# Attention with a memory state, then 128 chosen rows through two layers: full-array reads, a row of scores by way of DRAM, and two batches turned by VectorE

## The chip, the cores and the metric

The kernel runs on one core of a Trainium2 chip. A core has TensorE (matrix products, called PE in the profile), VectorE (DVE), ScalarE (ACT), GpSimd (POOL) and SyncE (SP), each with its own queue of instructions that it takes in order, and 16 DMA engines that they share. The metric is the device time of one execution in microseconds; the median of the runs counts.

## The reference

```
B, H, S, Ns, D = 8, 8, 512, 32, 64                  # all float32
scores = x @ state^T / 8                            # (B,H,512,32)
a  = softmax(scores) over the 32;   xread = a  @ state      # (B,H,512,64)
scores2 = state @ x^T / 8                           # (B,H,32,512)
a2 = softmax(scores2) over the 512; sread = a2 @ x          # (B,H,32,64)
X = concat(xread, sread) over rows, heads side by side      # (B,544,512)

s = X @ w_gate                                      # (B,544)
for each batch: take the 128 rows of largest s
    y = relu(rows @ w1) @ w2                        # 512 -> 1024 -> 512
    out[rows] = rows + sigmoid(s[rows]) * y
out elsewhere = X
```

Every batch goes through a small attention in both directions (each position reads the 32 states of its head, each state reads the 512 positions), and then 128 of its 544 rows go through two layers and are written back over themselves.

## The kernel before

A batch of x is loaded into one tile `xf` (partition p holds positions 4p to 4p+3 of every head). TensorE turns it, four transposes for each pair of heads (`turn`, L340), and ScalarE copies the turned blocks out of PSUM into `xT` (`turned`, L349). With the turned states as weights, 16 small matmuls give the scores of all heads in one PSUM tile `ps_s` (L369). VectorE turns the scores in 32 by 32 blocks, takes maximum, difference, sum and product over the 32 states and turns the result back (`in`, `max`, `sub`, `sum`, `mult`, `out`, L383 to L405; ScalarE does the exponential, L393). The other direction takes its exponential straight from PSUM (L415), is turned by TensorE (L469, kept by ScalarE at L472) and is multiplied with `xf` (`sread`, L485).

The read of a position (`read`, L447) is done in four chunks c of 128 positions. A chunk is four matmuls, for two groups g of four heads and two halves i of the array: 64 rows of weights (`eT`, half i) and 129 columns of `st_v`, in which two heads stand side by side and a last column holds the state's own gate score. They fill `ps_o`, two banks, of which there is one buffer. ScalarE copies the 512 columns to the tile `xs` (`rows`, L451), and VectorE adds the four gate columns to the scores `sc` of the chunk (`gate`, L455). `xs` is stored by SP (L512), and four small stores take the state rows (L517).

The choice of a batch needs its 544 scores as a row on every partition. TensorE transposes each column of `sc` spread over 128 columns (`row`, L558, and `row_s`, L561, for the last 32), and ScalarE copies the row to `srow` (L564, L567). VectorE counts for each row how many others beat it (`win`, L577, five operations), TensorE adds what is missing (`over`, L604), VectorE turns the rank into a one-hot matrix (`oh`, L617, five operations) and TensorE picks row numbers and scores with it (`pick`, L632). GpSimd fetches the chosen rows from `out` in DRAM (`fetch`, L524), which waits for that batch's stores. The layers run for batches [0], [1, 2], [3, 4], [5, 6] and [7]: transposes (L690, kept by ScalarE at L693), first layer (L707), second layer (L724), the sum on VectorE (L727) and the put into `out` by GpSimd (L524 again).

What runs when is a fixed order, written by a planner in `carry_out` (L112). Each piece of work is given its engine, a length, the pieces it comes after, the buffers it takes or uses, and a key: the batch number plus a number of its kind from the table `LATER`. The layers have 100 added there, so that TensorE takes them only where no attention piece is ready. The planner steps through time, and on the engine that is free first it takes, of the pieces that could start within `SOON` of the first, the one with the smallest key. A transfer has a time to landing (`lands`) that those after it wait for in the plan. On the chip each engine takes its own pieces in the planned order and waits for semaphores where a real duration differs from the planned one. SP's queue holds the loads, the stores and their waits in one order.

Of the kernel before, what the change touches and what calls it, by code (L numbers as in the profile page):

```python
# [18 lines left out]
def kernel(  # L19
# [35 lines left out]
    def pool(name, bufs, **kw):  # L55
        return ctx.enter_context(tc.tile_pool(name=name, bufs=bufs, **kw))

    N_X, N_XR = 5, 8
# [4 lines left out]
    psum = pool("psum", 1, space=bass.MemoryType.PSUM)  # L63

# [5 lines left out]
    SOON = {"PE": 0.0000, "DVE": 0.4931, "ACT": 0.0000, "POOL": 1.8045, "SP": 0.3000}  # L70

    LATER = {
        "add": -100.0000, "below": 1.9500, "exp": -0.0600, "exps": -0.7084, "fetch": 0.2600, "first": 100.0000,
        "gate": -0.5600, "gate_s": 4.8280, "heads": 0.4872, "in": -1.0433, "index": -2.8646, "load": -50.0000,
        "load_x": -2.0000, "max": 4.0896, "mult": 4.3959, "numbers": 0.2545, "off": -1.9260, "oh": -2.4538,
        "out": 3.4200, "over": -2.2366, "parts": -2.6851, "pick": 0.3200, "put": -100.0000, "read": 4.9387,
        "relu": -100.0000, "row": -4.7962, "row_kept": 4.8694, "row_s": -3.1695, "row_s_kept": -0.1742,
        "rows": 5.0000, "score_s": -3.7680, "scores": -1.0816, "second": 100.0000, "sexp": -0.1370,
        "sigmoid": 0.2238, "smax": 1.1888, "sread": 1.2957, "srows": -2.7199, "ssum": 1.4281, "state_T": 0.3300,
        "state_gates": 2.6509, "states": -1.3434, "store": 4.7700, "sub": -1.8119, "sum": -4.7918,  # L80
        "tables": -4.6345, "turn": -0.1899, "turn_a": 4.0218, "turned": 4.7352, "turned_a": -5.0000,
        "twice": -2.9080, "win": 4.2491, "xg": 90.0000, "xg_kept": -100.0000,
# [15 lines left out]
    class Piece:  # L98
        def __init__(self, engine, length, fn, after, takes, uses, key, lands):
            self.engine, self.length, self.fn, self.lands = engine, length, fn, lands  # L100
            self.name, self.key = key[1], key[0] + LATER.get(key[1], 0.0)
# [10 lines left out]
    def carry_out():  # L112
# [7 lines left out]
        while left:  # L120
# [15 lines left out]
            assert ready, "the plan cannot go on"  # L136
# [19 lines left out]
    P_O = Ring("ps_o", [128, 1024], F32, 1, psum)  # L156
    P_H = Ring("ps_h", [128, 512], F32, 2, psum)
    R_X = Ring("xf", [128, H, NC, D], F32, N_X, xin)
    R_XT = sbuf("xT", [128, 2, 2, 128], 12)
# [4 lines left out]
    R_XS = sbuf("xs", [128, NC, Dm], 2)  # L164
# [32 lines left out]
    st_v = const.tile([128, B, 2, 2 * D + 1], F32, name="st_v")  # L197
# [8 lines left out]
    st_T = const.tile([128, B, 2, 128], F32, name="st_T")  # L206
# [6 lines left out]
    def state_V(lo, hi):  # L213

        for q in range(4):
            k = q % 2
            r = slice(Ns * q, Ns * (q + 1))
            nc.gpsimd.tensor_copy(out=st_v[r, lo:hi, :, D * k:D * (k + 1)], in_=st_c[r, lo:hi, :, 0])
# [572 lines left out]
```

## Time and profile before

| what | value |
|---|---|
| median of three runs | 221.9 us (221.47 to 222.27) |
| the profiled execution, its own time | 222.47 us |
| its span | 220.7 us |
| granted TensorE clock | 0.999 |
| busy: TensorE, VectorE, ScalarE, GpSimd | 202.4, 124.5, 85.9, 49.9 us |
| moved by DMA | 26.59 MB, mean 120 GB/s |
| stores of `xs`, 1 MB each: issue to landing | 4.3 us (median of 8) |
| stores of state rows, 16 KB each | 2.1 us (median of 32) |

The profile is of one execution. Its span runs from the first to the last instruction; what lies around it makes the execution's own time longer. A group of instructions has its line in the kernel, its engine, its operation and tiles, its count, its busy time and the mean of one, and then the idle time of its engine just before it with what ended that. An fp32 matmul stands as two records, a transpose as one. Ends of matmuls are modelled, so neighbouring ones overlap; what one of a row costs is best read from the start of one to the start of the next.

### The profile page before, as it was taken

The page shows a single profiled execution, that of the slowest core. Times are in us where ns is not written, and L with a number is a line of the kernel's source. Part 1 is how long each engine was busy: PE and PEld are TensorE (multiplying, and loading weights), DVE is VectorE, ACT ScalarE, POOL GpSimd, SP SyncE. Part 2 cuts the span into 40 slices and gives each one's busy share as a digit, 9 for nine tenths or more (in the row PEclk, how much of TensorE's full clock was granted, in tenths as well). Part 3 has the DMA queues.
Part 4 walks back from the last instruction along what each step waited for, and adds up shares of the span by engine and source line. Part 5 has one row for each costly group of instructions (what it writes and reads, how often), then busy time and mean ns, then how long its engine had stood idle before and what let it go on. Part 6 is the DMA issues. An engine that isn't in the chain of part 4 may idle for free.

```text
span 220.7 us, 4784 instructions
## 1 busy us (share of the span) xinstructions
PE 202.4 (92%) x1928; PEld 142.4 (65%) x1928; DVE 124.5 (56%) x349; ACT 85.9 (39%) x172; POOL 49.9 (23%) x128
## 2 busy tenths in 40 slices
PE   2497898898999999999999999999999999999990
PEld 2355675676878954778886455888645788447840
DVE  3159989987887897798868896730062100011001
ACT  3139878778776315453725133323301021100200
POOL 7229001041105124110142423301035200011001
PEclk9999999999999999999999999999999999999999
DMA  6999969826314301150050711502212000010001
GB/s 213 329 306 402 369 207 288 305 54 205 131 74 157 111 0 48 52 196 9 34 207 13 238 50 49 239 3 95 95 48 94 33 19 0 0 50 11 36 0 48
DMA packets 17406, 26.59 MB, mean 120 GB/s; under 512 B 5608, under 2 KB 13800, under 8 KB 16360
## 3 DMA queue, kind: packets, MB, share of 16 engines
q1 hardware_dynamic: 15032, 21.43, 28.0%
q0 software_dynamic: 1280, 4.20, 6.1%
q10 hardware_dynamic: 1072, 0.66, 0.9%
q8 instruction: 15, 0.25, 0.5%
q14 instruction: 7, 0.06, 0.1%
HBM read 15.27 MB, written 11.01 MB: 119 GB/s over the span
## 4 chain that ended last, share of the span: by engine, by line
PE 55%; issue 20%; DMA 8%; POOL 6%; ACT 5%; DVE 2%; POOLq 1%; ACTq 0%
PE ps_h L707 17%; PE ps_h L724 12%; PE ps_o L447 7%; DMA out_dram<-xs 4%; PE ps_tr L340 4%; PE ps_s L369 3%; DMA xf<-in_state_dram 3%; PE ps_tr L469 3%; PE ps_tr L485 3%; ACT a L415 2%; POOL out_dram L524 2%; PE ps_tr L604 2%; PE ps_tr L558 2%; POOL xr L524 1%; ACT xT L349 1%
## 5 line engine op out<-in xcount | busy, mean ns | idle before, releaser
L707 PE MATMUL ps_h<-xg,w 128*128 128x256 f32 (+1 forms) x320 | 60.4, 341 | 0.0
L724 PE MATMUL ps_h<-w,hT 128*128 128x512 f32 x128 | 58.9, 601 | 0.0
L707 PEld LDWEIGHTS ps_h<-xg,w 128*128 128x128 f32 x320 | 50.3, 191 | 5.9 <-issue 0.5
L724 PEld LDWEIGHTS ps_h<-w,hT 128*128 128x128 f32 x128 | 23.1, 190 | 23.2 <-issue 22.5
L340 PE MATMUL ps_tr<-ident,xf 128*128 128x128 f32 x128 | 21.5, 311 | 9.7 <-DMA xf<-in_x_dram 4.1
L727 DVE SCALAR_TENSOR_TENSOR ot<-ps_h,z,xr 128x512 f32<-128x512 f32 x8 | 6.0, 749 | 43.1 <-PE ps_h L724 43.1
L451 ACT COPY xs<-ps_o 128x512 f32<-128x512 f32 x32 | 18.8, 586 | 28.2 <-PE ps_o L447 14.1
L711 ACT ACTIVATE hT<-ps_h 128x512 f32<-128x512 f32 x16 | 9.5, 596 | 49.7 <-PE ps_h L707 49.7
L340 PEld LDWEIGHTS ps_tr<-ident,xf 128*128 128x128 f32 x128 | 15.5, 156 | 14.8 <-issue 5.3
L577 DVE SCALAR_TENSOR_TENSOR win<-srow,sc,after 128x544 bf16<-128x544 f32 (+4 forms) x40 | 18.3, 501 | 8.4 <-ACT srow L567 8.4
L447 PE MATMUL ps_o<-st_v,eT 64*128 64x129 f32 x256 | 22.9, 297 | 0.1
L447 PEld LDWEIGHTS ps_o<-st_v,eT 64*128 64x128 f32 x256 | 16.8, 186 | 6.0 <-issue 2.8
L349 ACT COPY xT<-ps_tr 128x512 f32<-128x512 f32 x30 | 16.8, 589 | 9.6 <-PE ps_tr L340 9.6
L524 POOL DMA_INDIRECT out_dram<-ot,idx x8 | 8.4, 1047 | 53.2 <-DVE ot L727 51.0
L524 POOL DMA_INDIRECT xr<-out_dram,idx x8 | 8.5, 1057 | 48.1 <-DVE idx L637 16.3
L588 POOL CAST aux<-sc 128x5 bf16<-128x5 f32 x8 | 1.9, 232 | 52.3 <-DVE sc L455 38.3
L455 DVE TENSOR_REDUCE sc<-ps_o 128x1 f32<-128x4 f32 x32 | 5.1, 158 | 12.1 <-PE ps_o L447 7.0
L415 ACT ACTIVATE a<-ps_s,nm 128x512 f32<-128x512 f32 x16 | 10.9, 689 | 2.0 <-DVE nm L411 2.0
L383 DVE STREAM_TRANSPOSE e<-ps_s 128x1024 f32<-128x1024 f32 x8 | 10.0, 1247 | 2.9 <-PE ps_s L369 2.9
L369 PE MATMUL ps_s<-xT,st_T 64*32 64x256 f32 x256 | 9.6, 413 | 1.7 <-ACT a L415 1.7
L469 PE MATMUL ps_tr<-ident,a 128*128 128x128 f32 x64 | 10.2, 284 | 1.1 <-ACT a L415 0.5
L397 DVE TENSOR_REDUCE sm<-e 128x32 f32<-128x1024 f32 x8 | 9.7, 1210 | 1.5 <-ACT e L393 1.5
(84 smaller groups left out, 229.9 us busy)
## 6 DMA issues: line engine op xcount, KB each, us to landing
out_dram<-xs SPq DMA_DIRECT2D x8, 1024.0 KB, 4.3
xf<-in_x_dram SPq DMA_DIRECT2D x14, 512.0 KB, 6.8
w<-in_moe_w_dram SPq DMA_DIRECT2D x2, 2048.0 KB, 10.1
xf<-in_x_dram SPq DMA_DIRECT2D x2, 256.0 KB, 3.2
xf<-in_x_dram ACTq DMA_DIRECT2D x2, 256.0 KB
out_dram<-xt SPq DMA_DIRECT2D x32, 16.0 KB, 2.1
xf<-in_state_dram SPq DMA_DIRECT2D x1, 384.0 KB
xf<-in_state_dram ACTq DMA_DIRECT2D x1, 128.0 KB, 7.1
```

What stands on the lines that cost most here:

```text
L340: nc.tensor.transpose(v[:, k, r], xf[b].ap[:, 2 * pair + k, 2 * r:2 * r + 2].rearrange("p w d -> p (w d)"), ident)
L349: nc.scalar.copy(out=t.ap, in_=v)
L369: nc.tensor.matmul(view_s()[Ns * q:Ns * (q + 1), w, g], st_T[half, b, g, Ns * q:Ns * (q + 1)], xT[2 * g + q // 2].ap[half, q % 2].rearrang ...
L383: nc.vector.transpose(out=flat(e), in_=s.ap)
L415: nc.scalar.activation(out=a.ap[:, g], in_=view_s()[:, :, g], func=AF.Exp, bias=tmp["nm"][:, g:g + 1], accum_out=tmp["ss"][:, g:g + 1])
L447: nc.tensor.matmul(view(o)[:, i, g, 0:2 * D + 1], eT.ap[half, c % 2, g, c // 2], st_v[half, b, g], start=True, stop=True)
L451: nc.scalar.copy(out=xs.ap[:, c].rearrange("p (g i m) -> p g i m", g=2, i=2), in_=view(o)[:, :, :, 0:2 * D].rearrange("p i g m -> p g i m"))
L469: nc.tensor.transpose(v[:, c], a.ap[:, g, c % 2, 128 * (c // 2):128 * (c // 2 + 1)], ident)
L524: touches(b, nc.gpsimd.indirect_dma_start(**kw), True)
L577: nc.vector.scalar_tensor_tensor(wins[c].ap[0:n], srow.ap[0:n, f:SP], sc[0:n, b, c:c + 1], after[0:n, 0:SP - f], op0=ALU.is_gt, op1=ALU.mu ...
L707: nc.tensor.matmul(v[:, f, 0:n], w1[:, j, 128 * (f0 + f):128 * (f0 + f + 1)], xg.ap[:, j, 0:n], start=(j == 0), stop=(j == ND - 1))
L724: nc.tensor.matmul(py.ap[0:m], hT.ap[:, f, lo:lo + m], w2[:, f], start=(f == 0), stop=(f == NF - 1))
```

## The change

**Reads.** `st_v` becomes block-diagonal over all four heads of a group (4 x 64 columns and the gate column), so that a chunk and group need one matmul on the full array with 257 columns in place of two half-array ones with 129. `ps_o` is one bank with two buffers; ScalarE copies 257 columns, gate column included, for each of the 64 pairs of batch, chunk and group, and one operation of VectorE per batch adds the gate columns from `xs`.

**Row of scores.** For batches 1 to 7 the scores are stored to a small DRAM tile (`row_out`: one transfer for the 512, one for the 32), and SP reads them back spread over 128 partitions (`row_in`). Batch 0 keeps the transposes.

**x of batches 6 and 7.** A second copy of x, cut so that blocks of 32 positions by 32 of the head's numbers lie on one partition group, is loaded into `x2` (one buffer, four transfers in pieces of 32 numbers), after the scores of the batch two before. VectorE turns it in 32 by 32 blocks straight into `xT` (`blocks`), and TensorE's transposes and ScalarE's copies of these batches fall away. `xf` is loaded as before for `sread`.

**One-hot.** The five operations become one over 5 x 128 columns, from offsets in one of two fixed tiles.

**Planner.** All of `LATER` and two of `SOON` have new values, pieces of batch 0 get a key of -3 in place of 0, a plan that cannot go on falls back to the written order, `xT` has 8 buffers for 12 and `xr` 6 for 8, and a turn takes its `xT` buffer at the transposes and not only at the copy.

```diff
@@ -55,31 +55,36 @@
     def pool(name, bufs, **kw):
...
-    N_X, N_XR = 5, 8
+    N_X, N_XR = 5, 6
+    BY_DRAM = range(1, B)
+    ON_DVE = (6, 7) if cap <= 128 else ()
+    DV = 4 * D + 1
...
+    dram = pool("dram", 1, space=bass.MemoryType.DRAM)
...
-    SOON = {"PE": 0.0000, "DVE": 0.4931, "ACT": 0.0000, "POOL": 1.8045, "SP": 0.3000}
+    SOON = {"PE": 0.0000, "DVE": 0.3346, "ACT": 0.0000, "POOL": 1.5570, "SP": 0.3000, "DMA": 0.0000}
+    EARLY = -3.0
...
@@ -98,7 +103,7 @@
     class Piece:
         def __init__(self, engine, length, fn, after, takes, uses, key, lands):
...
-            self.name, self.key = key[1], key[0] + LATER.get(key[1], 0.0)
+            self.name, self.key = key[1], (key[0] or EARLY) + LATER.get(key[1], 0.0)
@@ -133,7 +138,9 @@
-            assert ready, "the plan cannot go on"
+            if not ready:
+                order = pieces
+                break
@@ -153,15 +160,17 @@
-    P_O = Ring("ps_o", [128, 1024], F32, 1, psum)
+    P_O = Ring("ps_o", [128, 512], F32, 2, psum)
...
-    R_XT = sbuf("xT", [128, 2, 2, 128], 12)
+    R_XT = sbuf("xT", [128, 2, 2, 128], 8)
+    R_X2 = sbuf("x2", [128, 2, H, 4, 32], 1)
...
-    R_XS = sbuf("xs", [128, NC, Dm], 2)
+    R_XS = sbuf("xs", [128, NC, 2, 4 * D + 4], 2 if cap <= 128 else 1)
+    R_SD = Ring("scores_d", [SP], F32, 2, dram)
@@ -194,7 +203,7 @@
-    st_v = const.tile([128, B, 2, 2 * D + 1], F32, name="st_v")
+    st_v = const.tile([128, B, 2, DV], F32, name="st_v")
@@ -204,6 +213,7 @@
+    offs = [const.tile([128, NC + 1], F32, name=f"off{i}") for i in range(2)]
@@ -213,9 +223,8 @@
     def state_V(lo, hi):
...
-            k = q % 2
...
-            nc.gpsimd.tensor_copy(out=st_v[r, lo:hi, :, D * k:D * (k + 1)], in_=st_c[r, lo:hi, :, 0])
+            nc.gpsimd.tensor_copy(out=st_v[r, lo:hi, :, D * q:D * (q + 1)], in_=st_c[r, lo:hi, :, 0])
...
     def twice(lo, hi, engine):
@@ -228,7 +237,7 @@
-        nc.vector.reduce_sum(out=st_v[:, lo:hi, :, 2 * D], in_=t, axis=AX.X)
+        nc.vector.reduce_sum(out=st_v[:, lo:hi, :, 4 * D], in_=t, axis=AX.X)
...
     def pool_tables():
@@ -243,6 +252,8 @@
+        for off in offs:
+            nc.gpsimd.memset(off, 0.0)
...
     def row_numbers():
@@ -254,7 +265,7 @@
-    xf, p_x, last_load = {}, {}, []
+    xf, p_x, last_load, x2, p_x2, p_scores = {}, {}, [], {}, {}, {}
...
     def load_x(b, key, pieces=2):
@@ -272,6 +283,20 @@
+    def load_x2(b, key):
...
+        buf = x2[b] = Buf(R_X2)
+        p_x2[b] = []
+        for w in range(2):
+            for e in range(2):
+                def go(w=w, e=e):
+                    src = x[b].rearrange("h (s t r w) (e d) -> w e t r h s d", s=4, t=32, r=2, e=2)[w, e]
+                    o = 32 * (2 * w + e)
+                    nc.sync.dma_start(out=buf.ap[o:o + 32], in_=src)
...
+                p_x2[b].append(add("SP", 0.65, go, after=[p_scores[b - 2]], takes=[] if p_x2[b] else [buf],
+                                   uses=[buf] if p_x2[b] else [], key=key, lands=4.0))
...
     def load(on, length, fn, uses=()):
@@ -339,6 +364,14 @@
+            if b in ON_DVE:
+                def turn_blocks(pair=pair, t=t):
+                    nc.vector.transpose(out=t.ap.rearrange("p k r t -> p r k t"),
+                                        in_=x2[b].ap[:, :, 2 * pair:2 * pair + 2].rearrange("p r k s d -> p r k (s d)"))
...
+                p_xT.append(add("DVE", 0.64, turn_blocks, after=p_x2[b], takes=[t], uses=[x2[b]], key=key("blocks")))
+                xT.append(t)
+                continue
...
             def keep(ps=ps, t=t, on=on):
@@ -349,10 +382,10 @@
-            p = add("PE", 0.47 if b else 0.9, turn, after=[px[(pair * len(px)) // (H // 2)]] + last_turn[-1:], takes=[ps], uses=[xf[b]],
+            p = add("PE", 0.62 if b else 0.9, turn, after=[px[(pair * len(px)) // (H // 2)]] + last_turn[-1:], takes=[ps, t], uses=[xf[b]],
...
-            p_xT.append(add(on, 0.6, keep, after=[p], takes=[t], uses=[ps], key=key("turned")))
+            p_xT.append(add(on, 0.6, keep, after=[p], uses=[ps, t], key=key("turned")))
@@ -370,7 +403,7 @@
-        p_s = add("PE", 1.02, scores, after=p_xT + [p_sT[b]], takes=[s], uses=xT, key=key("scores"))
+        p_s = p_scores[b] = add("PE", 1.09, scores, after=p_xT + [p_sT[b]], takes=[s], uses=xT, key=key("scores"))
@@ -433,31 +466,25 @@
-        p_xs, p_sc = [], []
+        p_xs = []
...
-            o = Buf(P_O)
...
-            def view(o):
-                return o.ap.rearrange("p (i g m) -> p i g m", i=2, g=2)
...
-            def read(c=c, o=o):
-                for g in range(2):
-                    for i in range(2):
-                        half = slice(D * i, D * (i + 1))
-                        nc.tensor.matmul(view(o)[:, i, g, 0:2 * D + 1], eT.ap[half, c % 2, g, c // 2], st_v[half, b, g],
-                                         start=True, stop=True)
...
-            def keep(c=c, o=o):
-                nc.scalar.copy(out=xs.ap[:, c].rearrange("p (g i m) -> p g i m", g=2, i=2),
-                               in_=view(o)[:, :, :, 0:2 * D].rearrange("p i g m -> p g i m"))
...
-            def gate(c=c, o=o):
-                nc.vector.tensor_reduce(out=sc[:, b, c:c + 1], in_=view(o)[:, :, :, 2 * D], axis=AX.XY, op=ALU.add)
...
-            p = add("PE", 0.66, read, after=[p_eT, p_pool[b], p_sg[b]], takes=[o], uses=[eT],
-                    key=key("read"))
-            p_sc.append(add("DVE", 0.15, gate, after=[p, p_tab], uses=[o], key=key("gate")))
-            p_xs.append(add("ACT", 0.6, keep, after=[p], takes=[] if c else [xs], uses=[o] + ([xs] if c else []), key=key("rows")))
+            for g in range(2):
+                o = Buf(P_O)
...
+                def read(c=c, g=g, o=o):
+                    nc.tensor.matmul(o.ap[:, 0:DV], eT.ap[:, c % 2, g, c // 2], st_v[:, b, g], start=True, stop=True)
...
+                def keep(c=c, g=g, o=o):
+                    nc.scalar.copy(out=xs.ap[:, c, g, 0:DV], in_=o.ap[:, 0:DV])
...
+                p = add("PE", 0.22, read, after=[p_eT, p_pool[b], p_sg[b]], takes=[o], uses=[eT], key=key("read"))
+                p_xs.append(add("ACT", 0.37, keep, after=[p], takes=[xs] if not p_xs else [], uses=[o] + ([xs] if p_xs else []),
+                                key=key("rows")))
...
+        def gate():
+            nc.vector.reduce_sum(out=sc[:, b, 0:NC], in_=xs.ap[:, :, :, 4 * D], axis=AX.X)
...
+        p_sc = [add("DVE", 0.15, gate, after=p_xs + [p_tab], uses=[xs], key=key("gate"))]
@@ -471,7 +498,7 @@
             def keep(ps=ps, t=t):
...
-            p = add("PE", 0.5, turn, after=[p_a[g]], takes=[ps, t], uses=[a], key=key("turn_a"))
+            p = add("PE", 0.62, turn, after=[p_a[g]], takes=[ps, t], uses=[a], key=key("turn_a"))
@@ -509,7 +536,7 @@
     def store_base(b, xs, tmp, p_xs, p_xt):
         def x_rows():
-            touches(b, nc.sync.dma_start(out=out[b, 0:S].rearrange("(p c) m -> p c m", c=NC), in_=xs.ap))
+            touches(b, nc.sync.dma_start(out=out[b, 0:S].rearrange("(p c) (g m) -> p c g m", c=NC, g=2), in_=xs.ap[:, :, :, 0:4 * D]))
...
         def s_rows():
@@ -560,12 +587,27 @@
         def row_s():
...
-        p = add("PE", 0.55, row_x, after=p_sc, takes=[ps1], key=key("row"))
-        p_r1 = add("ACT", 0.59, lambda: nc.scalar.copy(out=srow.ap[:, 0:S], in_=ps1.ap), after=[p], takes=[srow],
-                   uses=[ps1], key=key("row_kept"))
-        p = add("PE", 0.2, row_s, after=[p_ss, p], takes=[ps2], key=key("row_s"))
-        p_r2 = add("ACT", 0.2, lambda: nc.scalar.copy(out=srow.ap[:, S:SP], in_=ps2.ap[:, 0:Ns]), after=[p, p_r1],
-                   uses=[srow, ps2], key=key("row_s_kept"))
...
+        scores_d = Buf(R_SD)
...
+        def row_out():
+            with nc.allow_non_contiguous_dma(reason="scores by place"):
+                nc.sync.dma_start(out=scores_d.ap[0:S].rearrange("(c p) -> p c", c=NC), in_=sc[:, b, 0:NC])
+                nc.sync.dma_start(out=scores_d.ap[S:SP].rearrange("(p c) -> p c", c=1), in_=sc[0:Ns, b, NC:NC + 1])
...
+        def row_in():
+            nc.sync.dma_start(out=srow.ap, in_=scores_d.ap.unsqueeze(0).to_broadcast([128, SP]))
...
+        if b in BY_DRAM:
+            p = add("SP", 1.2, row_out, after=p_sc + [p_ss], takes=[scores_d], key=key("row_out"), lands=2.0)
+            p_r1 = p_r2 = add("SP", 0.6, row_in, after=[p], takes=[srow], uses=[scores_d], key=key("row_in"), lands=2.2)
+        else:
+            p = add("PE", 0.62, row_x, after=p_sc, takes=[ps1], key=key("row"))
+            p_r1 = add("ACT", 0.59, lambda: nc.scalar.copy(out=srow.ap[:, 0:S], in_=ps1.ap), after=[p], takes=[srow],
+                       uses=[ps1], key=key("row_kept"))
+            p = add("PE", 0.2, row_s, after=[p_ss, p], takes=[ps2], key=key("row_s"))
+            p_r2 = add("ACT", 0.2, lambda: nc.scalar.copy(out=srow.ap[:, S:SP], in_=ps2.ap[:, 0:Ns]), after=[p, p_r1],
+                       uses=[srow, ps2], key=key("row_s_kept"))
@@ -605,20 +647,19 @@
         def offsets():
-            off = tmp["off"] = small.tile([128, NC + 1], F32, name="off")
+            off = offs[b % 2]
...
         def one_hot():
-            for c in range(NC + 1):
-                m = rows[c]
-                nc.vector.tensor_scalar(oh.ap[0:m, c], places[0:m, c], tmp["off"][0:m, c:c + 1], None, op0=ALU.is_equal)
+            nc.vector.tensor_tensor(out=oh.ap, in0=places, in1=offs[b % 2].unsqueeze(2).to_broadcast([128, NC + 1, n_slots]),
+                                    op=ALU.is_equal)
...
-        p_oh = add("DVE", 1.06 * n_slots / 128, one_hot, after=[p], takes=[oh], key=key("oh"))
+        p_oh = add("DVE", 0.1 + 0.72 * n_slots / 128, one_hot, after=[p], takes=[oh], key=key("oh"))
@@ -744,6 +785,8 @@
+        if b in ON_DVE:
+            load_x2(b, (b, "load_x2"))
...
```

A line of "..." stands for lines left out: unchanged ones, and the rows of numbers in `LATER`.

More of the change, by code (lines that the diff above doesn't have):

```diff
@@ L63 @@
     psum = pool("psum", 1, space=bass.MemoryType.PSUM)
+    dram = pool("dram", 1, space=bass.MemoryType.DRAM)
     ctx.enter_context(tc.manual_schedule(engines={ENG.PE, ENG.DVE, ENG.Activation, ENG.SP, ENG.Pool}))
     HOP = 0.1
-    SOON = {"PE": 0.0000, "DVE": 0.4931, "ACT": 0.0000, "POOL": 1.8045, "SP": 0.3000}
+    SOON = {"PE": 0.0000, "DVE": 0.3346, "ACT": 0.0000, "POOL": 1.5570, "SP": 0.3000, "DMA": 0.0000}
+    EARLY = -3.0
     LATER = {
[L73 to L82, printed above, removed]
@@ new lines @@
+        "add": -100.0000, "below": 5.0000, "blocks": 2.1051, "exp": -0.1136, "exps": 4.8094, "fetch": -0.6907,
+        "first": 100.0000, "gate": -0.7843, "gate_s": 4.2011, "heads": 4.3136, "in": 5.0000, "index": -4.4535,
+        "load": -50.0000, "load_x": -2.0000, "load_x2": -4.7068, "max": 1.7089, "mult": 2.6844, "numbers": 3.8624,
+        "off": -5.0000, "oh": -4.0291, "out": -2.6823, "over": -1.8313, "parts": -1.4386, "pick": -0.9186,
+        "put": -100.0000, "read": 1.7224, "relu": -100.0000, "row": 4.4529, "row_in": -2.5757, "row_kept": 1.5458,
@@ new lines @@
+        "row_out": 0.8175, "row_s": -0.2014, "row_s_kept": 4.3591, "rows": 3.6389, "score_s": -4.1248,
+        "scores": 3.1842, "second": 100.0000, "sexp": -3.2482, "sigmoid": 1.1072, "smax": -0.3926, "sread": -0.6531,
+        "srows": -2.7900, "ssum": -4.6931, "state_T": -3.4100, "state_gates": -4.7374, "states": 3.1826,
+        "store": -4.9572, "sub": 2.4861, "sum": 0.6863, "tables": 1.9575, "turn": -3.6599, "turn_a": 4.7706,
+        "turned": 3.8922, "turned_a": -3.7562, "twice": 3.5213, "win": 2.4128, "xg": 90.0000, "xg_kept": -100.0000,
```

## The prediction

> **What bounds the kernel now.** I read the page's busy times and slices first, then stretches of the span, then the groups with shapes kept apart, and last the chain of waits. The page says which engine is full and when:
>
> ```profile
> PE 202.4 (92%) x1928; PEld 142.4 (65%) x1928; DVE 124.5 (56%) x349; ACT 85.9 (39%) x172; POOL 49.9 (23%) x128
> ...
> PE   2497898898999999999999999999999999999990
> ```
>
> The stretches split this (columns: stretch, length, then busy time of PE, PEld, DVE, ACT and POOL):
>
> ```profile
> 60.00:90.00 30.00, 29.17 (x399) 21.43 (x398) 25.12 (x77) 15.26 (x32) 8.18 (x20) 1.00 0.25 87
> 90.00:165.00 75.00, 74.96 (x619) 52.61 (x619) 50.12 (x166) 26.32 (x53) 16.45 (x52) 1.00 0.26 95
> ```
>
> From 90 us on TensorE never stops; before that VectorE is almost as full (25.1 of 30 us), and TensorE fills waits with early turns of x and with the layers of batch 0. TensorE is idle for 220.7 - 202.4 = 18.3 us: 6.9 in the first ten, about 1 in each ten up to 60, 0.8 between 80 and 90, 5.6 after its last matmul. So the end is TensorE's work plus its idle time; work taken away after 90 us counts in full, work taken from the filled waits before it may only become idle time.
>
> What a piece costs is in the chain (start, duration, what), here inside the full stretch:
>
> ```profile
> 137.22 0.65 PE ps_o L447 x8
> 137.86 1.92 PE ps_h L707 x8
> 139.79 0.44 PE ps_tr L558 x4
> 140.22 0.17 PE ps_tr L561
> 140.39 1.92 PE ps_h L707 x8
> 142.32 0.65 PE ps_o L447 x8
> 142.96 0.59 PE ps_tr L690 x4
> 143.55 1.73 PE ps_h L707 x8
> ```
>
> A read of one chunk (L447, half-array, eight records for four matmuls) takes 0.65 us. The piece after it pays too: four L707 matmuls take 1.92 us after a read or after the 32-row L561, and 1.73 us after full-array transposes; L690 takes 0.59 after a read, where L558, four transposes as well, takes 0.44 after a layer. So a change of tile shape costs the follower 0.15 to 0.19.
>
> The prices of the rest (busy us, mean ns of one):
>
> ```profile
> L340 PE MATMUL ps_tr<-ident,xf 128*128 128x128 f32 x128 | 21.5, 311 | 9.7 <-DMA xf<-in_x_dram 4.1 <-DVE xT L347 2.9 <-ACT xT L349 2.0
> L451 ACT COPY xs<-ps_o 128x512 f32<-128x512 f32 x32 | 18.8, 586 | 28.2 <-PE ps_o L447 14.1 <-DVE sc L455 13.7 <-DVE rs L420 0.3
> L405 DVE STREAM_TRANSPOSE eT<-e 128x1024 f32<-128x1024 f32 x8 | 9.9, 1236 | 0.1
> L455 DVE TENSOR_REDUCE sc<-ps_o 128x1 f32<-128x4 f32 x32 | 5.1, 158 | 12.1 <-PE ps_o L447 7.0 <-ACT xs L451 4.9
> ```
>
> **What the Trainium skill says.** "TensorEngine Tiling (Array Packing)", Key Properties: changing the tiling mode, not just the tile, drains TensorE. The trace agrees: 0.15 to 0.19 us on the follower. "DMA: Bandwidth & Descriptors", Anatomy of one DMA, gives a fixed cost of about 2 us however small the transfer; here 16 KB stores land in 2.1 us (median). Its Rules for kernel authors say that a non-contiguous last dimension becomes one descriptor per element, which is the stored row (512 floats, then 32); no run here shows 4-byte packets. "VectorE: DVE Perf Modes" has two-tensor operations in fp32 at one element a cycle; the trace's 1.21 us for 1024 elements agrees.
>
> **The change, part by part.**
>
> Reads. 32 chunks x 0.65 = 20.8 us go, and 64 full-array matmuls of 257 columns come. The nearest row is L707 with 256 columns: 1.73 / 4 = 0.43 us, so 0.434 each, 27.8 in all: +7.0. (The plan's own length for them, 0.22, is half of that; it is about one of the two records of a matmul.) But 25 of the 32 reads are followed in the timeline by a full-array piece, which then no longer pays about 0.17: -4.3. Net +2.7. Bounds: +7.0 if the followers pay on, +2 if the other seven gain too.
>
> Row of scores. In seven batches L558 (0.62, 0.58 and five times 0.44, together 3.4), L561 (7 x 0.17 = 1.2) and its charge on six followers (6 x 0.19 = 1.1) go: -5.7. All of them start after 57 us, where TensorE is full.
>
> Turns. Batch 7's four pairs (0.58 + 0.58 + 1.02 for two, at 55 to 60 us) go: -2.2. Batch 6's go too, -2.1, but they stood at 42 to 47 us, where each waited for a copy: little else was ready.
>
> TensorE in sum: +2.7 - 5.7 - 4.3 = -7.3 us, so 195.1.
>
> ScalarE. A copy of 257 columns costs, on the line from 32 columns (0.193) to 512 (0.586), 0.377; 64 make 24.1 for 18.8: +5.4. Row copies go, 7 x 0.78 = -5.5, and eight turned copies, -4.7. It has room: 39% busy.
>
> VectorE. Gates: 32 x 0.158 become 8 x 0.16, -3.8. The one-hot: five operations, 1.06 together, become one over 640 elements; from 0.918 at 768 and 1.211 at 1024 that is 0.77: 8 x -0.29 = -2.3. Blocks: eight half-size L405, 0.65 each: +5.2. In sum -0.9, but the 5.2 fall before 95 us, where VectorE is nearly full, and the savings of that stretch, about four batches x 0.8, are 3.2: +2 there.
>
> Transfers. The row now needs two issues (1.2), a landing (2.1), another issue (0.6) and a landing (2.1): 6.0 us instead of about 1.5 by TensorE and ScalarE. SP stands still between the two; stores, x2 and later rows queue behind it. The store of 1 MB lands in 4.3, so a row behind it loses some 3 more. Against that, the reads had one ps_o, and their copies came about 2.1 us apart (28.6, 30.9, 33.2, 35.0 us in batch 0); with two buffers eight copies need about 4 us, which gives back some 4 to 5. So the choice of a batch comes about 3 us later. The wait falls on the five window operations: behind them on VectorE stand the softmax steps of later batches, and for those TensorE waits.
>
> x2 is 8192 packets of 128 bytes a batch, in four issues of about 0.6. The nearest case is the state load in 256-byte packets:
>
> ```profile
> DMA packets 834, 0.27 MB, mean 272 GB/s; under 512 B 755, under 2 KB 834, under 8 KB 834
> ```
>
> This is one microsecond (12 to 13) of 16 engines: 19 ns a packet. At that rate x2 takes 9.8 us, at 437 GB/s by bytes 2.4, and about 2 on top: 4.5 to 12. I take 9; the plan counts on 6.6. x2 of batch 6 is asked for after scores of batch 4 (51 us before), that of batch 7 after blocks of 6 and scores of 5 (60 us); their scores came at 81 and 96. That cover hides it unless the blocks stand early in VectorE's order: then all behind them waits, at most 5.4 us each.
>
> Stores now go in 1 KB pieces instead of 8 KB ones; I cost that at nothing, because the layers wait for no store after the first, and at up to 1 us each otherwise. GpSimd clears twice as many columns of `st_v` (1.39 and 0.52 us become about 2.8 and 1.0); the first read came at 27.9 us, long after, so nothing, and 1.9 us at the start if not. The new order values move pieces among engines; that I cannot price and put at -2 to +3.
>
> **Sum.** Work 195.1. Idle time 18.3, plus 2.1 for batch 6's turns which become idle, plus 1 because the layers of batch 0 are used up before those of 1 and 2 are ready (their rows come 3 us later, TensorE has some 70% attention work meanwhile), plus 1 of late transfers: 22.4. Span 217.5. The profiled execution took 222.47, 1.8 above its span of 220.7, and 0.6 above the median of 221.9: so 219.3 for a like execution, 218.7 for the median.
>
> **The rivals.**
>
> A (forecast, 0.44): as summed, 216 to 220.5. For it: nothing but TensorE sets the end from 90 us on.
>
> B (0.34), slower: transfers land later than the plan thinks while VectorE's order is fixed. At 12 us, x2 is 5.4 late, twice 10.8. In the stretch before 95 us about three quarters pass to TensorE, 8 us instead of the 1 counted: span 224.6, median 226. It decides from 3.2 us more idle time than I count. For it: VectorE is 84% busy there, and the x2 loads, stores and rows share one SP queue. Against it: 20 to 30 us between request and scores.
>
> C (0.14): no gain. Follower charges stay (+4.3): 195.1 becomes 199.4, median 223 with my idle time, 222 with one microsecond less.
>
> D (0.06): all of the 7.3 comes through and the single ps_o's end makes the early stretch 1 us shorter: 213.5.
>
> E (0.02): the changed planner may give up and run the written order (`order = pieces`). Then layers no longer fill waits, and the time is far above 227.
>
> **How the numbers follow.** Runs of before lie 221.47 to 222.27, so 0.3% (0.7 us) is about what can be told from no change. Faster: A and D, 0.50. Same: most of C, 0.10. Slower: B, E and the rest of C, 0.40. Leaving out E, the far side of B and half of D gives 214 to 227; signs being mixed, A's own 216 to 220.5 stands beside it. The time is A's.
>
> **What would show it.** Right: reads of two records with about 217 ns from one to the next, layer pieces after them at 1.73; TensorE busy about 195; no L558 but batch 0's; idle before 95 us up by 4. Wrong: VectorE waiting for x2 or for the row before 95 us for more than 4 us in all; follower pieces still at 1.92; layers of batches 1 and 2 starting after 95 us with a gap before them (89.7 now).

## The result and the profile after

The changed kernel took 296.2 us (median of four runs, 294.3 to 297.9) where the kernel before took 222.1 beside it (221.5 to 223.4): the ratio is 1.333, with a 95% interval of 1.321 to 1.344. The forecast was 218.7, its range 214 to 227. A few single executions, of the kernel before too, were over 1.5% slower than the fastest of their kernel, and the medians below leave them out.

In the page of the changed kernel, the busy times and the slices with TensorE's clock:

```profile
PE 218.4 (74%) x1733; PEld 153.0 (52%) x1733; DVE 126.1 (43%) x301; ACT 80.9 (27%) x182; POOL 52.0 (18%) x130
...
PE   3577988657850699917919990999739369999992
...
PEclk9999999959976599985977996699968859999999
```

TensorE, which before was busy from 90 us to its last matmul, now has holes from 60 to 240 us. Its idle time is 295.5 - 218.4 = 77.1 us, where it was 18.3: +58.8. Its busy time rose too, 202.4 to 218.4, though it has less to do. The clock row goes with it: from 59 us on the granted clock falls in and after each hole (its mean is 0.884, before 0.999). In finer stretches of the same trace TensorE does nothing from 88 to 98 us, the clock stands at 0.50 from 92 to 104 and at 1.00 again from 106. Matmuls of the layers' second half took 652 ns at the mean where they took 601. "TensorE: Matmul & The Clock Gate", Part 1, of the Trainium skill says that idleness throttles the array; this trace agrees. Span: 58.8 + 16.0 = 74.8 us more.

The stretches of the changed kernel (stretch, length, busy time of PE, PEld, DVE, ACT, POOL, then clock, DMA share and GB/s), to set against 29.17 and 74.96 of before:

```profile
60.00:90.00 30.00, 20.16 (x243) 16.14 (x242) 10.97 (x33) 7.42 (x16) 3.81 (x11) 0.83 0.68 131
90.00:165.00 75.00, 51.66 (x382) 37.36 (x383) 37.80 (x94) 19.02 (x46) 9.93 (x25) 0.80 0.43 67
```

VectorE fell most: from 25.1 busy us between 60 and 90 to 11.0. The waits of the changed kernel (engine, what waited, for what: us in total, times, longest) name what it waited for:

```profile
DVE win L619 <- DMA srow<-scores_d: 82.3, 7, 17.8
...
PEld L646 <- DVE win L619: 37.0, 16, 10.6
PE ps_tr L646 <- DVE win L619: 33.5, 14, 10.4
```

The window operations wait for the row of scores in every one of the seven batches that take it through DRAM, 11.8 us each time, and TensorE waits behind them. Before, this wait was 8.4 us over two batches; the line is from the waits of before:

```profile
DVE win L577 <- ACT srow L567: 8.4, 2, 8.1
```

The DMA issues of the changed kernel (number of issues, KB each, median us to landing) show why:

```profile
x<-in_x_dram SPq DMA_DIRECT2D x8, 256.0 KB, 6.9
srow<-scores_d SPq DMA_DIRECT2D x7, 272.0 KB, 4.3
...
xr<-out_dram,idx POOLq DMA_INDIRECT x8, 8.8
...
scores_d<-sc SPq DMA_DIRECT2D x7, 2.0 KB, 12.4
```

A store of 2 KB lands after 12.4 us and its read after 4.3; the sum counted 2.1 for each. GpSimd's fetch of the chosen rows went from 3.5 to 8.8 at the median. Its landings fall into groups: the three fetches issued together with a row's store or during it took 12.2 to 13.1 us, one beside the loads of x2 8.8, and three away from both 3.3 to 3.7 (of the eighth the trace has none). Here is one of the slow ones in the chain:

```profile
142.36 12.21 DMA xr<-out_dram,idx
```

And in SP's timeline the store beside it and the read that waits for this store:

```profile
142.45 0.37 SPq L595 DMA_DIRECT2D scores_d<-sc  x1
...
153.01 0.33 SPq L599 DMA_DIRECT2D srow<-scores_d  x1
```

The fetch starts with the store and lands at 154.6, 1.6 us after SP could go on. One pass of the chain (start, duration, what), at the longest wait:

```profile
76.19 5.35 SPq L296
...
81.63 2.32 SPq L595
...
83.99 8.88 DMA scores_d<-sc
...
92.92 4.26 DMA srow<-scores_d
...
97.20 1.82 DVE win L619 x6
...
99.07 0.27 PE ps_tr L646 x4
```

SP stands at the issue of x2 for batch 6 (L296); then comes the row's store (L595), 8.9 us of landing, and the row's read. VectorE's timeline shows that it did nothing meanwhile:

```profile
79.20 0.16 DVE L701 TENSOR_TENSOR z<-z 128x1 f32<-128x1 f32 x1
97.20 0.79 DVE L619 SCALAR_TENSOR_TENSOR win<-srow,sc,after 128x544 bf16<-128x544 f32 x1 [17.84 <-DMA srow<-scores_d]
```

Behind the window operation in its order stands the softmax of the next batch (the 1.21 us `nm` of L444 starts right after it, at 99.40), so the attention that should fill TensorE could not be made.

### The profile page after: what moved, and what is told of

Read it like the earlier page. It is cut to its first block, busy times and chain, and to the rows that moved or that the text cites. A ratio compares the mean times of both kernels' runs of the same rounds, so it can differ in the third digit from the quotient of the medians.

```text
span 295.5 us, 4404 instructions
## 1 busy us (share of the span) xinstructions
PE 218.4 (74%) x1733; PEld 153.0 (52%) x1733; DVE 126.1 (43%) x301; ACT 80.9 (27%) x182; POOL 52.0 (18%) x130
## 4 chain that ended last, share of the span: by engine, by line
DMA 35%; PE 24%; issue 16%; DVE 11%; POOL 5%; SPq 5%; ACT 1%; POOLq 0%; DVEq 0%; ACTq 0%
DMA scores_d<-sc 16%; DMA xr<-out_dram,idx 9%; PE ps_h L765 8%; PE ps_o L475 6%; DMA srow<-scores_d 5%; DVE win L619 4%; PE ps_h L748 3%; DMA xf<-in_x_dram 3%; DMA xf<-in_state_dram 3%; SPq L296 2%; PE ps_tr L646 2%; POOL st_v L227 1%; SPq L595 1%; PE ps_tr L512 1%; DVE eT L438 1%
## 5 line engine op out<-in xcount | busy, mean ns | idle before, releaser
L765 PE MATMUL ps_h<-w,hT 128*128 128x512 f32 x128 | 65.1, 652 | 0.0
L619 DVE SCALAR_TENSOR_TENSOR win<-srow,sc,after 128x544 bf16<-128x544 f32 (+4 forms) x40 | 18.2, 512 | 82.3 <-DMA srow<-scores_d 82.3
L478 ACT COPY xs<-ps_o 128x257 f32<-128x257 f32 x64 | 23.5, 379 | 61.9 <-PE ps_o L475 60.8
L475 PE MATMUL ps_o<-st_v,eT 128*128 128x257 f32 x128 | 38.5, 426 | 0.0
L646 PE MATMUL ps_tr<-ones,win 128*128 128x1 bf16 (+2 forms) x120 | 8.1, 170 | 34.7 <-DVE win L619 33.5
L475 PEld LDWEIGHTS ps_o<-st_v,eT 128*128 128x128 f32 x128 | 25.1, 211 | 6.5 <-issue 2.1
L646 PEld LDWEIGHTS <-win 128*128 128x128 bf16 (+2 forms) x120 | 6.4, 103 | 39.0 <-DVE win L619 37.0
L365 PE MATMUL ps_tr<-ident,xf 128*128 128x128 f32 x96 | 16.2, 317 | 9.6 <-DMA xf<-in_x_dram 5.3
L365 PEld LDWEIGHTS ps_tr<-ident,xf 128*128 128x128 f32 x96 | 12.2, 160 | 13.6 <-issue 4.4
L731 PE MATMUL ps_tr<-ident,xr 128*128 128x128 f32 x32 | 6.1, 326 | 17.2 <-DMA xr<-out_dram,idx 17.2
L731 PEld LDWEIGHTS ps_tr<-ident,xr 128*128 128x128 f32 x32 | 4.5, 164 | 19.5 <-issue 19.0
L512 PE MATMUL ps_tr<-xf,aT 128*32 128x64 f32 x512 | 9.5, 222 | 6.4 <-issue 4.9
```

The source lines that it names most:

```text
L365: nc.tensor.transpose(v[:, k, r], xf[b].ap[:, 2 * pair + k, 2 * r:2 * r + 2].rearrange("p w d -> p (w d)"), ident)
L475: nc.tensor.matmul(o.ap[:, 0:DV], eT.ap[:, c % 2, g, c // 2], st_v[:, b, g], start=True, stop=True)
L478: nc.scalar.copy(out=xs.ap[:, c, g, 0:DV], in_=o.ap[:, 0:DV])
L512: nc.tensor.matmul(o2.ap[rr, D * g:D * (g + 1)], aT[g].ap[:, c, rr], xf[b].ap[:, 4 * g + q, c], start=(c == 0), stop=(c == NC - 1))
L619: nc.vector.scalar_tensor_tensor(wins[c].ap[0:n], srow.ap[0:n, f:SP], sc[0:n, b, c:c + 1], after[0:n, 0:SP - f], op0=ALU.is_gt, op1=ALU.mu ...
L646: nc.tensor.matmul(ps3.ap[0:m, c:c + 1], wins[cc].ap[0:rows[cc], o:o + m], ones[0:rows[cc]], start=(cc == 0), stop=(cc == c))
```

## The experiments

**Theories.** R: the row's transfers are late, and the fixed orders pass the lateness on. X: x2 is late (rival B as priced). P: the changed order itself is bad (O in e1's expectation). Q: the row is late because it stands behind other transfers in SP's queue. Within R (T in the expectations): is it the 4-byte pieces, their number, or the plan that doesn't know of them? Ratios are to runs of the kernel before made beside each group, whose medians were 222.6 (e1 to e4), 222.6 (e5 to e8) and 222.4 (e9 to e12). Where no interval is given, there was one run.

**e1: all but the rows.** The changed kernel with rows by TensorE and ScalarE again.

```diff
-    BY_DRAM = range(1, B)
+    BY_DRAM = ()
```

> The changed kernel with one part undone: all batches get their row of scores by TensorE's transposes and ScalarE's copies, nothing by DRAM; reads, x2, one-hot and order values stay. Theory T (the 4-byte packets of the stored row make it land about 10 us late, and VectorE's fixed order waits for it, 82 us in all): the waits of the window operations fall below 15 us in all, TensorE is not idle for long and keeps its clock, time 215 to 228. Rival O (the new order values are a bad order whatever the transfers do): still above 250. Rival X (the x2 loads hold everything up): above 250 too, with long waits for x2.

228.2 us, ratio 1.024 [1.021, 1.027], at the upper end of what R expected; the window operations wait 10.1 us for their rows. So 68.0 of the loss goes with the rows, and what is left (full reads, x2, the one-hot and the new order) is slower than before too. TensorE is busy for 203.3 us at full clock. The chain of e1 in its full stretch prices the reads:

```profile
105.51 0.87 PE ps_o L475 x4
106.38 1.73 PE ps_h L748 x8
```

Two reads (four records) take 0.87, and the layer piece after them 1.73, as counted.

**e2: all but x2.** Rows by DRAM, batches 6 and 7 turned by TensorE.

```diff
-    ON_DVE = (6, 7) if cap <= 128 else ()
+    ON_DVE = ()
```

> The changed kernel with the other transfer undone: x of batches 6 and 7 is turned by TensorE, there is no x2; the row still goes by DRAM. Theory T: the row's store still lands in 9 us or more, window operations wait 60 us or more, time 275 to 300. Rival X or Q (the row is late because it stands behind x2 and the stores in SP's queue): for X the time falls below 250; for Q the rows of the two or three batches that had x2 ahead of them land in under 6 us.

288.9 us; the wait for the row is 69.2 us over seven times. X falls as the main cause: x2 adds 7.3 where the rows are late, and the loss stands without it. From the issue of a row's store to that of its read SP needs 12 to 14 us in all seven batches, so Q in the form of x2 ahead in the queue falls too.

**e3: the row in five packets.** One transpose (128 by 5) and one small copy turn the scores, and the row is stored as four runs of 512 bytes and one of 128; order values and read are as in the change.

```diff
-                nc.sync.dma_start(out=scores_d.ap[0:S].rearrange("(c p) -> p c", c=NC), in_=sc[:, b, 0:NC])
+                nc.sync.dma_start(out=scores_d.ap[0:S].rearrange("(c p) -> c p", c=NC), in_=scT.ap[0:NC])
...
+                nc.tensor.transpose(ps1.ap[0:NC + 1, 0:128], sc[:, b], ident)
```

> The changed kernel, but the scores of a batch are first turned by one transpose of TensorE (128 by 5) and copied by ScalarE, so that the row is stored in 5 packets of 512 and 128 bytes in place of 544 of 4; it is read back as before, behind the same stores and x2 loads. Theory T: the store lands in 2 to 4 us where nothing large is ahead of it, window operations wait 25 us or less, time 218 to 235. Rival Q (place in the queue, or the way by DRAM as such): it still lands in 8 us or more and the time stays above 265.

233.8 us, ratio 1.049 [1.042, 1.057]: 62.4 of the 68 are gone with the small pieces, though the way through DRAM, its two landings and SP's standstill remain. Its chain shows one store with little beside it and one behind other transfers:

```profile
58.29 1.05 DMA scores_d<-scT
59.40 4.97 DMA srow<-scores_d
...
74.78 4.02 DMA scores_d<-scT
...
78.95 3.07 DMA srow<-scores_d
```

VectorE still waits 20.1 us for rows, in five batches: the read of 272 KB takes 3 to 5 us, above the 2.1 counted.

**e4: the plan told of 11 us, by the store's landing.** In the plan, the row's store lands 11 us after it is issued.

```diff
-            p = add("SP", 1.2, row_out, after=p_sc + [p_ss], takes=[scores_d], key=key("row_out"), lands=2.0)
+            p = add("SP", 1.2, row_out, after=p_sc + [p_ss], takes=[scores_d], key=key("row_out"), lands=11.0)
```

> The changed kernel with one number of the plan changed: the planner is told that the row's store takes 11 us to land in place of 2; the work is the same. If the loss is the fixed order of VectorE: the window operations are put later and wait less than 30 us in all, time 230 to 255. If the loss is the latency itself, in the chain from a batch's scores to its layers: waits move to TensorE (for the fetched rows), time above 270.

296.6 us, and the order of every queue is that of the changed kernel. It missed, and the code says why: for a piece on the same engine the planner's `since` returns `done[q]`, the end of the issue, and not `end[q]`, which includes the landing. The store and its read both stand on SP, so the landing between them counts nothing in the plan, whatever number is written there. That later pieces wait in the plan for a landing, as the description of the kernel has it, holds only for pieces on another engine. By itself the run is one more of the changed kernel.

**e5: the plan told of it, by SP's time.**

```diff
-            p_r1 = p_r2 = add("SP", 0.6, row_in, after=[p], takes=[srow], uses=[scores_d], key=key("row_in"), lands=2.2)
+            p_r1 = p_r2 = add("SP", 11.0, row_in, after=[p], takes=[srow], uses=[scores_d], key=key("row_in"), lands=2.2)
```

> The changed kernel with one number of the plan changed: reading the row back (on SP, which stands still until the stored row has landed) is given 11 us of SP's time in place of 0.6. The plan does not count the landing of a transfer for a later piece on the same queue, so that the run told 11 us as a landing got the same order in every queue, and is a repeat of the changed kernel. Here the order does change; the work is the same. If the loss is the order (VectorE put to the window operations as if the row came in 4 us): they wait less than 35 us in all, time 230 to 262. If it is the latency itself, in the chain from a batch's scores to its layers and through SP's queue: above 275.

251.9 us. The wait of the window operations for the row has left the list of waits: the plan now puts other work of VectorE ahead of them. So 44 us of the 68 go with an order that knew nothing of the lateness, and 24 stay although it knows (one run). TensorE is busy 207.0 us of 250.1; what it waits for now in the waits of e5 is, among others, the fetch:

```profile
PE ps_tr L731 <- DMA xr<-out_dram,idx: 10.0, 2, 9.8
```

**e6: the store by itself.** To the kernel before, after its last store on SP, are added six stores into a scratch tensor in DRAM, each followed by a small read that waits for it. The first is shown as an example; the others take 128 or 32 partitions, or store whole rows.

```diff
+    def four_by_512(d):
+        nc.sync.dma_start(out=d[0:S].rearrange("(c p) -> p c", c=NC), in_=sc[:, B - 1, 0:NC])
...
+            nc.sync.dma_start(out=back, in_=buf.ap[0:Ns].rearrange("(p c) -> p c", p=1))
```

> The kernel before, with stores to a DRAM scratch tile added on SP after its last store, each followed by a small read of it, so that they run one after the other while DMA is otherwise quiet: 512 packets of 4 bytes, 128 of 4, 32 of 4, 128 of 16, 4 of 512, and 512 of 4 again. Nothing waits for them but the end of the kernel. Theory T (a cost per packet, of about 300 ns on each of 16 engines): 9 to 12 us, 3 to 5, 2 to 3, 3 to 5, about 2. If the late landing came from the stores and x2 ahead in the queue: all of them about 2 to 3 us. If 4-byte pieces cost by their size and not by their number: 128 of 16 bytes clearly below 128 of 4.

SP's timeline of e6 (start, issue time, line); the step from a `probe_d` line to the `back` line after it is issue and landing. L764 stores 128 pieces of 4 bytes, L770 128 of 16 bytes, L773 four of 512 bytes, L761 the 512 pieces of 4 bytes of the changed kernel:

```profile
166.87 0.34 SPq L764 DMA_DIRECT2D probe_d<-sc  x1
176.35 0.24 SPq L783 DMA_DIRECT2D back<-probe_d  x1
...
182.62 0.34 SPq L770 DMA_DIRECT2D probe_d<-sc  x1
184.48 0.23 SPq L783 DMA_DIRECT2D back<-probe_d  x1
184.75 0.25 SPq L773 DMA_DIRECT2D probe_d<-ident  x1
186.22 0.21 SPq L783 DMA_DIRECT2D back<-probe_d  x1
186.48 0.39 SPq L761 DMA_DIRECT2D probe_d<-sc  x1
195.64 0.22 SPq L783 DMA_DIRECT2D back<-probe_d  x1
```

The changed kernel's store takes 9.2 us where DMA moves nothing else (0 GB/s from 186.5 to 195.6); the first of the six, the same store right behind one of 1 MB, took 14.1 (152.5 to 166.6). The same 2 KB in 16-byte pieces take 1.9, in 512-byte pieces 1.5. A price per packet is refuted: 512 and 128 pieces of 4 bytes take the same (9.2 and 9.5), and 128 of 16 bytes a fifth of it. A quarter as many (32 pieces) took 5.7, with a put of GpSimd's beside them.

**e10: the distance between the pieces.** Again the kernel before with stores added. In SP's timeline L763, L766, L769 and L772 store 128 pieces of 4 bytes whose places in DRAM lie 4, 16, 64 and 512 bytes apart; L775 stores 128 pieces of 8 bytes side by side.

```diff
+        nc.sync.dma_start(out=d[0:128].rearrange("(p c) -> p c", c=1), in_=SRC4)
...
+        nc.sync.dma_start(out=d[0:2048].rearrange("(p c) -> p c", c=16)[:, 0:1], in_=SRC4)
```

> The kernel before with stores to a DRAM scratch tile on SP after its last store, one after the other: first 128 packets of 16 bytes side by side (behind the last 1 MB store, so its time means little), then 128 of 4 bytes with starts 4, 16, 64 and 512 bytes apart, then 128 of 8 bytes side by side. The first probe gave 9.4 us for 128 of 4 side by side and 1.9 for 128 of 16. If pieces of 4 bytes are slow as such: all four near 9. If it is that neighbouring pieces fall into the same small block of DRAM and wait for one another: 9 at 4 apart, less at 16, about 2 at 64 and 512, and 8 bytes side by side between 3 and 7.

```profile
157.77 0.34 SPq L763 DMA_DIRECT2D probe_d<-sc  x1
166.64 0.24 SPq L788 DMA_DIRECT2D back<-probe_d  x1
166.93 0.34 SPq L766 DMA_DIRECT2D probe_d<-sc  x1
170.88 0.24 SPq L788 DMA_DIRECT2D back<-probe_d  x1
171.18 0.33 SPq L769 DMA_DIRECT2D probe_d<-sc  x1
172.67 0.24 SPq L788 DMA_DIRECT2D back<-probe_d  x1
172.96 0.33 SPq L772 DMA_DIRECT2D probe_d<-sc  x1
175.63 0.24 SPq L788 DMA_DIRECT2D back<-probe_d  x1
175.93 0.33 SPq L775 DMA_DIRECT2D probe_d<-sc  x1
179.02 0.24 SPq L788 DMA_DIRECT2D back<-probe_d  x1
```

8.9 us at 4 bytes apart, 4.0 at 16, 1.5 at 64 and 2.7 at 512; 8 bytes side by side took 3.1. (The kernels' own times, 231.2 us for e6 and 227.4 for e10, hold the added stores.) The number and the size of the pieces are the same in the four cases and only the distance was changed: what costs is that neighbours lie close together in DRAM, and 64 bytes of distance are enough to end it. Each case ran once, one after the other, and the 4.0 may be too high: GpSimd's fetch and put passed beside it (127 GB/s from 167.0 to 170.8). Why 512 bytes took longer than 64 stays open. "DMA: Bandwidth & Descriptors", Specifications, says that a transfer below 512 bytes is done by read-modify-write. That such writes close together wait for each other would fit these numbers; it is an inference, and nothing here shows it directly.

**e7, e8: the reads.** e7 is the changed kernel with both transfers undone: full-array reads and the single one-hot in the new order.

```diff
-    BY_DRAM = range(1, B)
-    ON_DVE = (6, 7) if cap <= 128 else ()
+    BY_DRAM = ()
+    ON_DVE = ()
```

> The changed kernel with both transfers undone (rows by TensorE, no x2): full-array reads, the single one-hot operation and the new order values are left. If turning batches 6 and 7 by VectorE is worth its 4.3 us of TensorE: slower than the run with x2 and rows by TensorE (228.2) by 2 to 5 us, TensorE busy about 207. If that work only filled waits: within 1.5 us of it, or faster.

e8 is the kernel before, with its order values and the full-array reads (told to the plan as 0.43 each), and with fewer buffers of `xT` (10 for 12) and `xr` (6 for 8).

```diff
+                def read(c=c, g=g, o=o):
+                    nc.tensor.matmul(o.ap[:, 0:DV], eT.ap[:, c % 2, g, c // 2], st_v[:, b, g], start=True, stop=True)
```

> The kernel before, with its own order values, and the full-array reads alone (with their copies and the single gate sum; the reads are planned with 0.43 us, xT has 10 buffers and xr 6 to make room). If pieces that follow a read no longer pay the change of tile shape: TensorE busy 204 to 206, layer pieces after a read at 1.73, time up by 1 to 4 us (224 to 227). If they pay on: busy about 209, 1.92 after a read, time 228 to 231.

e7: 230.1 us, ratio 1.036 [1.028, 1.044]. e8: 236.2, ratio 1.062 [1.053, 1.071]. With the reads the kernel is slower in both orders, by 7.5 and 13.6 us, but neither run changes the reads alone: both have fewer buffers of `xT` and `xr`, and e7 the single one-hot and the new order as well. e8 missed both of its forecasts: layer pieces after a read take 1.73 in its chain, as in the first, TensorE is busy for 210.3 us, as in the second, and it is idle for 24.1 where before had 18.3, which neither had. Between e7 and e1, x2 takes 4.3 us of TensorE's work (207.6 to 203.3) and 1.9 us of time, just under the 2 to 5 that were expected if the work counts.

**e9: the rows alone.** The kernel before with the rows by DRAM as in the change, and nothing else.

```diff
+    BY_DRAM = range(1, B)
...
+            p = add("SP", 1.2, row_out, after=p_sc + [p_ss], takes=[scores_d], key=key("row_out"), lands=2.0)
+            p_r1 = p_r2 = add("SP", 0.6, row_in, after=[p], takes=[srow], uses=[scores_d], key=key("row_in"), lands=2.2)
```

> The kernel before with one part of the change alone: the rows of batches 1 to 7 stored in 4-byte pieces and read back by DRAM, planned as in the changed kernel. Theory T: this part alone makes nearly all of the loss, 270 to 300, window operations waiting 60 us or more in all. If the loss needs the other parts (x2 ahead in the queue, the new order values): below 250.

290.5 us, 68.1 above before, with the old order values. From the waits of e9:

```profile
DVE win L594 <- DMA srow<-scores_d: 74.3, 7, 16.5
```

P falls as the main cause: this one part makes the same loss, alone or last.

**e11: the row in five packets, alone and planned.** The kernel before with the row as in e3, and its read given 2.8 us of SP in the plan.

```diff
+                nc.sync.dma_start(out=scores_d.ap[0:S].rearrange("(c p) -> c p", c=NC), in_=scT.ap[0:NC])
...
+            p_r1 = p_r2 = add("SP", 2.8, row_in, after=[p], takes=[srow], uses=[scores_d], key=key("row_in"), lands=2.2)
```

> The kernel before with the rows of batches 1 to 7 by DRAM in 5 packets (one transpose of TensorE and one small copy of ScalarE ahead), SP's wait planned with 2.8 us; its own reads and order values. TensorE loses three transposes, the row of 32 and its charge on the follower in seven batches, about 4 us. If a row that comes about 4 us later is hidden in the full stretch: 218 to 222. If the longer chain from scores to layers or the store queue costs more: 223 to 232.

222.5 us, ratio 1.001 [0.998, 1.004]: no change, between the two forecasts. Busy times and waits of e11:

```profile
PE 199.0 (90%) x1900; PEld 139.4 (63%) x1900; DVE 124.8 (56%) x349; ACT 81.8 (37%) x165; POOL 52.0 (24%) x128
```

```profile
DVE win L603 <- DMA srow<-scores_d: 2.6, 1, 2.6
```

The row is hardly late any more, and TensorE's work fell by 3.4 us, but its idle time rose by 3.6 (220.9 - 199.0 = 21.9), so nothing is won. Between 87 and 96 us its timeline has waits for attention pieces of VectorE and ScalarE of 3.5 us in all, where before had 0.8. It is the best way of passing the row through DRAM that was run, and no better than before.

**e12: x2 and the single one-hot alone.** The kernel before with these two, and eight `xT` buffers instead of 12.

```diff
+    ON_DVE = (6, 7) if cap <= 128 else ()
...
+            nc.vector.tensor_tensor(out=oh.ap, in0=places, in1=offs[b % 2].unsqueeze(2).to_broadcast([128, NC + 1, n_slots]),
+                                    op=ALU.is_equal)
```

> The kernel before with x of batches 6 and 7 turned by VectorE from x2 and the single one-hot operation; its own reads, rows and order values (the two new pieces have the keys of the changed kernel, xT has 8 buffers). TensorE loses 4.3 us of turns. If half of that comes through, as between the runs without and with x2: 219 to 222. If waits for x2 on VectorE take it back: 223 to 230.

233.1 us, ratio 1.045 [1.036, 1.054], above both forecasts. Here are two stretches of e12:

```profile
60.00:90.00 30.00, 24.60 (x280) 16.79 (x278) 22.08 (x58) 11.14 (x23) 5.77 (x18) 1.00 0.35 114
90.00:165.00 75.00, 68.00 (x602) 48.18 (x603) 54.52 (x147) 26.43 (x52) 17.88 (x51) 0.93 0.34 91
```

TensorE is busy for 11.5 us less than before from 60 to 165 us (29.17 and 74.96 there), although the turns that went stood before 60. No wait for x2 is among the larger ones. TensorE's largest wait is for fetched rows, 7.2 us in two waits, and one of these fetches took 8.1 us beside the loads of x2. Which of the order, the fewer buffers and the late x2 makes the holes was not taken apart.

The steps from before to the changed kernel, along the runs:

| kernel | median us | step |
|---|---|---|
| before (beside e1) | 222.6 | |
| + reads, one-hot, new order (e7) | 230.1 | +7.5 |
| + x2 (e1) | 228.2 | -1.9 |
| + row by DRAM in 5 packets (e3) | 233.8 | +5.6 |
| row in 4-byte pieces, planned with 11 us (e5, one run) | 251.9 | +18.1 |
| row in 4-byte pieces, planned as in the change (after) | 296.2 | +44.3 |

## Why the prediction was wrong

**The row's path: the failed step.** "Two issues (1.2), a landing (2.1), another issue (0.6) and a landing (2.1): 6.0 us": the landing of the store was taken from 16 KB stores in packets of 256 bytes, with the remark that no run shows 4-byte packets, and then used without a bound above. It measured 12.4 us at the median in the changed kernel (9.2 by itself, e6), and the read 4.3 instead of 2.1: with the counted issues, 1.2 + 12.4 + 0.6 + 4.3 = 18.5 instead of 6.0. A fetch that met a row's store took 12 to 13 us instead of 3.5. The fixed cost of about 2 us that the prediction cites is given by its page for transfers issued by GpSimd; from SP, where the row goes, it fits 128 pieces of 16 bytes (1.9) and not those of 4. The count of pieces isn't the price either (e6, e10).

**What follows from a late row: also mis-sized.** "The choice of a batch comes about 3 us later" was priced as one microsecond of idle time. VectorE's order is fixed, and its window operations, 82.3 us of waits in all, hold the softmax behind them (the sign named for a wrong forecast, over 4 us of such waits before 95 us, was met by a wait of 11.7 us up to 68.15 and by most of the 17.8 up to 97.20); idle time of TensorE rose by 58.8. Two things multiplied the lateness: seven batches pay it one after another, and the plan counts the store's landing as nothing (e4), so that it puts the windows too early every time (44 of 68 us, e5). The prediction took the lengths from the plan, but not what `since` counts. And idle time costs twice, by the lower clock: busy time went up by 16.0 instead of down by 7.3.

**Rival B** had the mechanism and the place, late transfers behind a fixed order of VectorE on a shared SP queue, but named x2 as the late one and priced 8 us. The parts of x2 landed after 6.9 at the median, within its bounds, but its four issues for batch 6 held SP for 8.1 us (2.00 + 6.10 in the timeline, from 71.7 to 81.5) where 2.4 were counted, and the row's store stood behind them. It is worth +7.3 beside late rows (e2) and -1.9 without them (e7 to e1), and in the old order, with the one-hot and fewer buffers of `xT`, the kernel with it is 10.6 slower (e12). B's own sign came true, its size not. E, the written order, did not come: the layers still lie between attention pieces.

**Reads: the mechanism was right, the size not.** Two reads take 0.87, so +7.0 holds. The credit for followers, -4.3, does not: I took 0.17 from the chain for all 25. By starts in the timeline of before, most layer pieces after a read took 1.83 against 1.73, and transposes 0.49 against 0.44, so most followers paid 0.05 to 0.10. The 1.92 after a read stand where another read comes next: there a read and a layer piece by turns took 2.57 together, and take 2.60 in e1, so in such rows the credit was right. A read after or before another tile shape now pays instead, mostly 0.96 to 1.07 for 0.87. Net of x2's -4.3, e1 has 203.3 + 4.3 - 202.4 = +5.2 of TensorE's time, not +2.7; what the new order adds to it was not separated. Then idle time came on top, 22.0 in e1.

**Turns and the small prices were right.** x2 takes 4.3 off TensorE (e7 to e1), as summed. The one-hot took 0.83 (0.77 counted), a half-size block 0.69 (0.65), a copy of 257 columns 0.379 (0.377).

**`st_v` at nothing: likely wrong.** In the first 30 us TensorE has 18.5 busy us in e1, 21.1 before. GpSimd's clear at the start grew from 1.39 to 2.66 us, and the turns of the states behind it start 1.4 later. That this causes the 2.6 is argued, not shown.

**Signs.** All of A's gains rest on work leaving a full TensorE. Where such work left with nothing late (e11: -3.4 busy), the time did not move: idle time took its place, part of it in waits for attention pieces. "Work taken away after 90 us counts in full" was too strong, because the freed time needs work that is ready, and the order of the layers is fixed as well.

## What to carry to other kernels

Before a small tensor is passed through DRAM, look at how its pieces lie there: make the last dimension long by one transpose, because neighbouring 4-byte writes took six times as long as the same bytes in a few runs. (Pieces 64 bytes apart were stored as fast, but reading them back as a row was not run.) In a kernel with a planned order, read how the plan counts a landing between two pieces of one queue, and price a late transfer by what stands behind its consumer, times the number of batches. Work taken off the bounding engine was no gain where no other work was ready (e11).

## What was not expected of the hardware

- A store of 128 floats side by side from 128 partitions took 8.9 to 9.5 us, as long as 512 floats in four such strips (9.2). At a distance of 64 bytes it took 1.5 (e6, e10).
- A fetch of GpSimd's that is issued while such a store is under way lands late, mostly just after it: after 7.7 and 11.3 us in e9, where the other six fetches took 3.4 to 3.5; after 11.3 in e2, 6.4 to 11.8 in e5, and 9.1 in e10 beside a single store of 128 floats; after 12.2 to 13.1 in the changed kernel. Two fetches beside the loads of x2 took 8.8 (changed kernel) and 8.1 (e12), but those of e1 5.7 at most. Why they hold the fetch back is not shown.
- TensorE's granted clock fell to 0.80 over 90 to 165 us in a program of one core, while holes stood between its matmuls; in the kernel before it was 1.00 there.
